# Attention with two kinds of heads, then a gated two-layer product: a new order for the first quarter, mask matmuls in row halves, and row loads put ahead of their transposes

## The chip, the core and the metric

The kernel runs on one core of a Trainium2 chip. TensorE (PE in the profile) multiplies, VectorE (DVE), ScalarE (ACT) and GpSimd (POOL) do the elementwise work, SyncE (SP) only issues transfers. Each engine takes its own instructions in the order in which the program wrote them and waits on semaphores for the others; a transfer is issued from the queue of one engine and lands later. The metric is the time of one execution in device microseconds (us); lower is better.

## The reference

For 4 batches, 8 heads, 768 positions and 64 values per head:

```
scores = (q @ k^T) / 8
mask   = causal                                  for the "retrieval" heads 0, 2, 6
       = causal and (key < 4 or distance < 64)   for the five "streaming" heads
a      = softmax(scores where mask, else -1e9)
x      = a @ v, heads side by side: [3072, 512]
h      = x @ w_in            # 512 -> 2048
out    = (h * sigmoid(beta * h)) @ w_out         # 2048 -> 512, [3072, 512] float32
```

## The kernel before

**Tiling.** The heads go in four pairs per batch, and the 768 query positions in two halves of 384 (3 tiles of 128). A *unit* is one pair of heads for one half of one batch; there are 32, and four units make a *chunk* (8 chunks, 384 rows of the output each). Of a pair, one head lies in partitions 0 to 63 and the other in 64 to 127, so that the scores of both come from two matmuls on 64 rows each that use the two halves of TensorE's rows side by side.

**Stages of a unit.** Its queries and keys are brought to the form [values, positions]. For the first 12 units this is done by a cast to bf16 (`cast`, words `ck`/`cq` in the table below), three transposes on TensorE (`transpose_qk`, `tk`/`tq`, L322) and a copy out of PSUM (`copy_qk`, `kk`/`kq`); later chunks are loaded already cast, row by row, from POOL's queue (`load_rows`, L282, into the tiles `s0` and `s1`), and transposed by transfers from SP's queue (`transposes_dma`, L294 for the keys, L297 for the queries). Streaming heads need a few key and value blocks with the sink positions in front (`KO`, `VO`; words `ko`, `vo`). Then `steps_QK` writes the scores to a two-bank PSUM tile `sp` (L451), ScalarE takes their exponentials into `es` (L460), and `steps_PV` multiplies by the values (L532; the extra 65th column gives the row sums). `normalize` divides, giving `x`, which is transposed into `xT`.

**Masks.** Units 0 to 7 have their masks added before the exponential: a matmul with the identity puts -1e9 where a key must not count (L422, words `ad`), and the scores are accumulated on it. Unit 5 is an exception: its words `ma` multiply `es` by a 0/1 mask on VectorE, as all units from 8 on do (L478 and following).

**The two layers.** `steps_G1` gives 128 groups of four 384-wide matmuls (L600), each followed by a tanh on ScalarE (L605) and a gate on VectorE (L608); `steps_G2` gives the output in steps of four 512-wide matmuls (L653). Groups 0 to 3 of chunk 0 read the first quarter of `w_in`, groups 4 to 7 the second. The quarters come by transfers from POOL's queue (L140, words `wi0` to `wi3`; `w_out` by `wo0` to `wo3`, L144).

**What sets the order.** All engines are scheduled by hand: instructions are issued as the program is written. `RAMP` is a list of words that writes out the work of units 0 to 7 and what goes between; `do(word)` turns each into instructions. `zz3` issues three 512-wide matmuls on zeros (`keep_busy`, L513) and `idle(9, ...)` nine more at the start (L167); they compute nothing. `lq1.0g` loads queries and keys of chunk 1, `lv` values, `mm`/`mA`/`mb` feed one step of the two layers, and a last letter v, a or g names the engine VectorE, ScalarE or GpSimd. `PLAN` has one row per unit from 8 on: V is a visit (scores and exponentials of two or three tiles), p a step of products with the values, a, A and b a step of the layers. `later(delay, fn)` puts smaller work (row loads, casts of values, masks) on a heap that `step` empties by a running estimate of TensorE's time.

## Time and profile before

| what | us |
|---|---|
| time, median of 3 runs (lowest, highest) | 228.91 (228.22, 229.04) |
| span of the profiled execution, first to last instruction | 227.0 |
| TensorE busy in it | 219.4 (97%) |
| ScalarE, VectorE, GpSimd busy | 154.0, 142.1, 87.3 |

The profiled execution's own time is not shown apart from its span; the median of the runs is 1.9 us longer than that span. In the profile's rows "busy" of TensorE counts a matmul from its start to the end of its result, so matmuls that follow each other overlap, and the distance from start to start is the better price of one. In rows of the timeline the first number is the start, the second the time covered, and a bracket tells how long the engine stood idle and what ended it.

### The profile page before, as it was taken

To read this page: it belongs to the slowest core of one execution; us is meant where nothing else is said; L and a number is where in the kernel's file an instruction comes from. 1 tells how busy PE (TensorE), PEld (TensorE's weight loads), DVE (VectorE), ACT (ScalarE), POOL (GpSimd) and SP (SyncE) were. 2 spreads that over 40 slices of the span, in tenths; PEclk is the share of its full clock that TensorE was granted. 3 is DMA by queue.
4 is the path that set the end of the run, shared out by engine and by line. 5 is a ranking of instruction groups with operands and counts; after the bars stand their busy time and mean duration, and the time that the engine had idled before them with its cause. 6 is when DMAs were issued, how large, how long until landed. Compare 5 with 4: busy or idle time off the path is not lost.

```text
span 227.0 us, 5019 instructions
## 1 busy us (share of the span) xinstructions
PE 219.4 (97%) x1898; PEld 126.4 (56%) x1917; DVE 142.1 (63%) x342; ACT 154.0 (68%) x254; POOL 87.3 (38%) x143
## 2 busy tenths in 40 slices
PE   7989999999999999999999999999999999999994
PEld 3555766654655665556654664556645655456553
DVE  4679888852684779357932699646963779028600
ACT  2698898946767897449933887569876878139621
POOL 5377952249163399143064049910670000000000
PEclk9999999999999999999999999999999999999999
DMA  6999999999999899989869779596963030111012
GB/s 204 262 301 239 225 197 198 195 220 171 149 216 178 161 153 144 141 175 133 103 131 162 126 151 140 92 133 103 216 64 107 24 81 0 49 46 46 0 49 92
DMA packets 95383, 31.66 MB, mean 139 GB/s; under 512 B 81776, under 2 KB 92416, under 8 KB 95360
## 3 DMA queue, kind: packets, MB, share of 16 engines
q1 hardware_dynamic: 58880, 22.82, 50.2%
q0 software_dynamic: 35904, 8.13, 41.9%
q10 hardware_dynamic: 576, 0.40, 0.6%
q8 instruction: 15, 0.25, 0.5%
q14 instruction: 8, 0.07, 0.1%
HBM read 27.27 MB, written 6.29 MB: 148 GB/s over the span
## 4 chain that ended last, share of the span: by engine, by line
PE 89%; DMA 4%; DVE 2%; SPq 2%; issue 1%; ACT 0%; ACTq 0%; DVEq 0%
PE mm L653 34%; PE mm L600 25%; PE sp L600 12%; PE sp L451 6%; PE po L532 6%; DMA s<-in_k_dram 3%; DMA s<-in_q_dram 2%; PE mm L638 2%; DVE es L478 1%; PE mm L322 1%; SPq L132 1%; PE mm L570 1%; PE mm L451 1%; SPq L119 1%; PE sp L422 1%
## 5 line engine op out<-in xcount | busy, mean ns | idle before, releaser
L653 PE MATMUL mm<-w_out_sb,gT 128*128 128x512 bf16 x349 | 84.1, 379 | 1.3 <-issue 0.5
L460 ACT ACTIVATE es<-sp 128x768 bf16<-128x768 f32 (+2 forms) x72 | 56.5, 837 | 19.6 <-PE sp L451 19.4
L600 PE MATMUL mm<-xT,w_in_sb 128*128 128x384 bf16 x348 | 64.6, 326 | 0.0
L600 PEld LDWEIGHTS <-w_in_sb 128*128 128x128 bf16 x512 | 47.8, 98 | 29.7 <-issue 0.2
L605 ACT ACTIVATE th<-mm,beta_h 128x384 f32<-128x384 f32 x87 | 49.8, 588 | 5.6 <-PE mm L600 0.9
L653 PEld LDWEIGHTS <-gT 128*128 128x128 bf16 x368 | 33.4, 98 | 36.0 <-issue 1.5
L608 DVE SCALAR_TENSOR_TENSOR gT<-th,mm 128x384 bf16<-128x384 f32 x87 | 46.8, 551 | 7.4 <-ACT th L605 3.8
L282 POOL DMA_DIRECT2D s<-in_q_dram x30 | 22.4, 761 | 27.2 <-DMA QTD<-s 21.7
L600 PE MATMUL sp<-xT,w_in_sb 128*128 128x384 bf16 x164 | 32.3, 326 | 0.0
L657 ACT ACTIVATE osb<-mm 128x512 f32<-128x512 f32 x23 | 13.8, 602 | 26.1 <-PE mm L653 25.8
L532 PEld LDWEIGHTS <-es 128*128 128x128 bf16 x472 | 23.3, 98 | 13.6 <-issue 1.5
L608 DVE SCALAR_TENSOR_TENSOR gT<-th,sp 128x384 bf16<-128x384 f32 x41 | 22.3, 552 | 5.6 <-ACT th L605 3.7
L532 PE MATMUL po<-VX,es 128*128 128x65 bf16 x360 | 24.9, 194 | 0.8 <-ACT VX L251 0.4
L605 ACT ACTIVATE th<-sp,beta_h 128x384 f32<-128x384 f32 x41 | 23.8, 586 | 2.3 <-PE sp L600 0.2
L282 POOL DMA_DIRECT2D s<-in_k_dram x30 | 22.4, 759 | 6.8 <-DMA w_out_sb<-in_moe_w_out_dram 5.2
L251 POOL CAST VX<-vs 128x512 bf16<-128x512 f32 x16 | 10.6, 662 | 34.6 <-DMA vs<-in_v_dram 31.8
L541 DVE RECIPROCAL rec<-po 128x6 f32<-128x6 f32 x28 | 5.4, 193 | 27.0 <-PE po L532 27.0
L478 DVE TENSOR_TENSOR es<-es,Mh 128x768 bf16<-128x768 bf16 (+1 forms) x26 | 17.4, 698 | 5.0 <-ACT es L460 4.4
L451 PE MATMUL sp<-QTD,KT 64*128 64x128 bf16 (+2 forms) x258 | 19.2, 240 | 0.6 <-ACT QTD L333 0.3
L545 DVE TENSOR_TENSOR x<-po,rec 128x384 bf16<-128x384 f32 x28 | 15.6, 557 | 1.0
L451 PEld LDWEIGHTS <-KT 64*128 64x128 bf16 x278 | 11.1, 94 | 5.8 <-issue 3.6
L259 POOL COPY VO<-VX 128x512 bf16<-128x512 bf16 x16 | 10.0, 649 | 7.3 <-DVE VX L251 7.3
(74 smaller groups left out, 157.2 us busy)
## 6 DMA issues: line engine op xcount, KB each, us to landing
vs<-in_v_dram SPq DMA_DIRECT2D x24, 256.0 KB, 5.5
out_dram<-osb SPq DMA_DIRECT2D x23, 256.0 KB, 2.8
w_in_sb<-in_moe_w_in_dram POOLq DMA_DIRECT2D x4, 512.0 KB, 9.7
w_out_sb<-in_moe_w_out_dram POOLq DMA_DIRECT2D x4, 512.0 KB, 16.5
s<-in_k_dram POOLq DMA_DIRECT2D x30, 64.0 KB, 4.8
s<-in_q_dram POOLq DMA_DIRECT2D x30, 64.0 KB, 5.1
s<-in_k_dram SPq DMA_DIRECT2D x4, 384.0 KB, 6.8
s<-in_q_dram SPq DMA_DIRECT2D x4, 384.0 KB, 8.6
```

Source lines behind the costliest of these rows:

```text
L251: copy(out=VX[b % 2][:, h2 * HT + t, :, 0:D], in_=staged["v", c][:, t])
L282: nc.gpsimd.dma_start(out=ROWS[c % 2, name][:, t, i * 4 * D:(i + 1) * 4 * D].rearrange("p (h d) -> p h d", d=D), in_=src[b, i:H:2, r:r + 1 ...
L451: nc.tensor.matmul(sps[i][r][:, x * 128:y * 128], key(a, lhs), s["QT"][half(a), qi * 128:(qi + y - x) * 128], start=first, stop=first or y ...
L460: nc.scalar.activation(out=views[i].rearrange("p r k j -> p r (k j)"), in_=banks[2][:, :, 0:n * 128], func=ACTF.Exp, scale=scale)
L478: nc.vector.tensor_mul(ev[:, :, 0:n], ev[:, :, 0:n], Mh[h2][:, None, m0:m0 + n].to_broadcast([128, 2, n, 128]))
L532: nc.tensor.matmul(po[:, qi, hh, :], e, val, start=(j == 0), stop=(j == len(lst) - 1))
L545: nc.vector.tensor_mul(xg[g][:, :, :, u % 2, :].rearrange("p a t d -> p t a d"), po[:, :, :, 0:D], rec.to_broadcast([128, HT, 2, D]))
L600: nc.tensor.matmul(hp[:, 0:HALF], w_in_sb[:, mo, fi * 128:(fi + 1) * 128], xT[c][:, mo, :], start=(mo == 0), stop=(mo == MO - 1))
L605: nc.scalar.activation(out=th, in_=hp[:, 0:HALF], func=ACTF.Tanh, scale=beta_h[:, fi:fi + 1])
L608: nc.vector.scalar_tensor_tensor(out=gTs[c][:, fi, :], in0=th, scalar=1.0, in1=hp[:, 0:HALF], op0=ALU.add, op1=ALU.mult)
L653: nc.tensor.matmul(op, gTs[c][:, fi, ns * 128:(ns + 1) * 128], w_out_sb[:, fi, :], start=(fi == 0), stop=(fi == FO - 1))
L657: nc.scalar.activation(out=osb, in_=op, func=ACTF.Copy, scale=0.5)
```

## The change

The first part of the program is written anew. The main points, with the names of the diff:

- Casts: the first units cast keys and queries in one instruction (`cast_both`, word `cb`), and all casts now run over heads outermost.
- Masks of units 0 to 7 (now unit 5 too): the -1e9 patterns are built on GpSimd in four kinds (`Nq`), folded into halves of 64 partitions (`Nt`, word `fo`), and added by matmuls of 64 columns (or two times 64) on 64 rows, alternating between the two row halves. The 0/1 masks that later units use are built later, on GpSimd (`late_masks`, word `mh`).
- Matmuls on zeros: five at the start (`zi5`) and 18 by `zz`, where there were nine and nine; the tile of zeros is smaller.
- `RAMP` and `PLAN` have their words in another order, and of the weights the third quarter of `w_in` goes ahead of, and the fourth behind, the first quarter of `w_out`.
- `transposes_dma` first issues all row loads of its chunk that are still on the heap. Before, four row loads of queries of chunk 6 and three of chunk 7 were still there when the transposes that read them were issued.
- `transpose_two` and `copy_two` are new, and no word of the table calls them.

```diff
+    def late_masks(part):
+        if part == 0:
+            nc.gpsimd.memset(Mh[0][:, 0:3], 1.0)
+            nc.gpsimd.memset(Mc, 1.0)
...
+    def folded(some, copy):
+        for r in range(2):
+            for h in range(2):
+                copy(out=Nt[64 * r:64 * r + 64, h, some], in_=Nq[64 * h:64 * h + 64, some])
...
-        copy(out=s["qkb"][:, "qk".index(name)], in_=staged[name, c, p // 2][:, p % 2:4:2].rearrange("p h t d -> p t h d"))
+        copy(out=s["qkb"][:, "kq".index(name)].rearrange("p t h d -> p h t d"), in_=staged[name, c, p // 2][:, p % 2:4:2])
...
+        for f in due_rows.pop(c, []):
+            f()
         for t in range(HT):
...
+    def cast_both(u, copy):
+        c, p = u // NPAIR, u % NPAIR
+        s = st_u.setdefault(u, {})
+        s["qkb"] = att.tile([128, 2, HT, 2, D], BF16, name="qkb", bufs=4)
+        copy(out=s["qkb"].rearrange("p i t h d -> p i h t d"), in_=both_of[c, p // 2][:, :, p % 2:4:2])
...
-                neg = Nc[:, 0:n * 128] if m is None else Ns[:, m * 128:(m + n) * 128]
-                nc.tensor.matmul(sps[i][r][:, 0:n * 128], ident, neg, start=True, stop=False)
+                kinds = [(0, 0, n)] if m is None else [((2, 3, 1, 3, 1)[m + x], x, 1) for x in range(n)]
+                todo.append([(r, h, *y) for y in kinds for h in range(2)])
                 covered[i, r] = n
+            opened_ = set()
+            while any(todo):
+                for some in todo:
+                    if some:
+                        r, h, kind, x, n = some.pop(0)
+                        rows_ = slice(64 * r, 64 * r + 64)
+                        nc.tensor.matmul(sps[i][r][:, x * 128:(x + n) * 128].rearrange("p (n j) -> p n j", n=n)[:, :, 64 * h:64 * h + 64], Nt[rows_, h, kind],
+                                         ident[rows_, None, 64 * r:64 * r + 64].to_broadcast([64, n, 64]), start=(r not in opened_), stop=False)
+                        opened_.add(r)
...
-        ck0g ne1 lv0.0 lv0.1 tk0 ck2a ne0 cq0v ck1a zz3 tq0 kq0a zz3 ad0.0 on0v lv0.2 kk0v cq1v tq1 qk0.0 tk2 ad0.1
+        zi5 cb0v cb1v zz1 zz2 zz3 fo0a lv0.0 ne0 tq0 fo1v tq1 tk0 zz1 lv0.1 zz2 lv0.2 kk0v tk1 zz1 ck3v lq1.0g zz2
+        be kq1a ad0.1 cb2v ad0.0 kq0a cq3a qk0.0 cv0.0v zz2 qk0.1 kk1a tq2 on0v kq2v cv0.1v zz2 ko1 tk2 cv0.2v vo0
...
-                later(1000 + 1500 * x, f)
+                due_rows.setdefault(c, []).append(later(1000 + 1500 * x, f))
```

Three places show how instructions moved; numbers behind a name tell buffers apart.

At the program's start VectorE before has these rows (`Mh`, `Ns`, `Mc` are masks, `qkb` the cast queries and keys, `s` the loaded ones):

```order
L150 MEMSET warm 1x1
L157 MEMSET zeros 128x256
L161 CAST idb<-idf 128x128
L177 MEMSET Mh_129 128x384
L193 TENSOR_SCALAR Ns<-Mh_129 128x256
L191 TENSOR_SCALAR Mc<-Nc 128x128
L193 TENSOR_SCALAR Ns<-Mh_129 128x384
L246 CAST qkb<-s_87 128x384
L228 MEMSET VX_145 128x48
L229 MEMSET VO_147 128x32
L330 COPY KT_149<-mm 128x384
```

And in the change:

```order
L149 MEMSET zeros 128x64
L155 MEMSET warm 1x1
L164 CAST idb<-idf 128x128
L328 CAST qkb<-s_89 128x2x2x3x64 x2
L212 COPY Nt<-Nq 64x384 x4
L377 COPY KT_126<-mm 128x384
L264 CAST qkb<-s_94 128x2x3x64
L742 TENSOR_SCALAR beta_h<-mm 128x16
```

The first masks left VectorE, the first two casts take four tiles each, and four copies that fold masks stand between them and the first copy of transposed keys.

GpSimd, around the transfers of the second quarter of `w_in`, before (the casts are those of chunk 1's last unit):

```order
L228 MEMSET VX_146 128x48
L229 MEMSET VO_148 128x32
L246 CAST qkb<-s_244 128x384
L312 COPY KO_156<-KT_150 128x128
L312 COPY KO_157<-KT_150 128x128
L140 DMA w_in_sb<-in_moe_w_in_dram 128x4x512 x3
L251 CAST VX_146<-vs 128x8x64
```

And in the change:

```order
L328 CAST qkb<-s_273 128x2x2x3x64
L173 AFFINE_SELECT Mh_111<-Mh_111 128x2x128
L173 AFFINE_SELECT Mh_111<-Mh_111 128x128
L187 MEMSET Mh_111 4x256
L359 COPY KO_133<-KT_127 128x128
L359 COPY KO_134<-KT_127 128x128
L173 AFFINE_SELECT Mh_111<-Mh_111 128x2x128
L173 AFFINE_SELECT Mc<-Mc 128x128
L253 COPY Mh_111<-Mh_111 128x256
L141 DMA w_in_sb<-in_moe_w_in_dram 128x4x512 x2
L269 CAST VX_123<-vs 128x8x64
L145 DMA w_out_sb<-in_moe_w_out_dram 128x4x512
```

The building of the 0/1 masks moved into this stretch, ahead of the second and third quarters of `w_in`, and the first of `w_out` took the fourth quarter's place.

SP, the transposes of chunk 6 before, with the semaphores that each row waits for (DMASW are those of POOL's row loads):

```order
L294 DMA_TRANSPOSE KT_149<-s_665 128x4x128 [waits DMAHW0_49,DMASW7_49,DMASW1_49]
L297 DMA_TRANSPOSE QTD_144<-s_643 128x4x128 [waits DMASW3_49,DMAHW1_49,DMASW2_49,PE_49]
L297 DMA_TRANSPOSE QTD_144<-s_643 128x4x128 [waits DMAHW2_49,PE_49]
L297 DMA_TRANSPOSE QTD_144<-s_643 128x4x128 [waits DMAHW3_49,PE_49]
L132 DMA vs<-in_v_dram 128x8x64 [waits DMAHW4_49]
```

And in the change:

```order
L316 DMA_TRANSPOSE KT_126<-s_624 128x4x128 [waits DMAHW2_49,DMASW1_49,DMASW0_49]
L319 DMA_TRANSPOSE QTD_121<-s_779 128x4x128 [waits DMASW3_49,DMAHW3_49,DMASW2_49,PE_49]
L319 DMA_TRANSPOSE QTD_121<-s_779 128x4x128 [waits DMASW5_49,DMAHW4_49,DMASW4_49,PE_49]
L319 DMA_TRANSPOSE QTD_121<-s_779 128x4x128 [waits DMASW7_49,DMAHW5_49,DMASW6_49,PE_49]
L133 DMA vs<-in_v_dram 128x8x64 [waits DMAHW6_49]
```

All three transposes of queries now wait for row loads, where two did not.

More of the change, by code (lines that the diff above doesn't have):

```diff
@@ L145, in load_w_out @@
         w_done.add(i)
+    zeros = consts.tile([128, 128], BF16, name="zeros")
+    nc.vector.memset(zeros, 0.0)
+    still = zeros[:, None, :].to_broadcast([128, 4, 128])
     load_qk(0, 0, 2)
@@ L166, in idle @@
             nothing = pool.tile([128, 512], F32, name=name)
-            nc.tensor.matmul(nothing, zeros[:, 0:128], zeros, start=True, stop=True)
-    idle(9, ps_m, "mm")
+            nc.tensor.matmul(nothing.rearrange("p (n j) -> p n j", n=4), zeros, still, start=True, stop=True)
     def select(buf, cm, step_, base, n):
@@ L448, in rows @@
                 seq = runs[0] + runs[1]
+            ends = {r: (r, x, y) for r, x, y, e in seq}
             for r, x, y, (a, lhs, qi, val, diag, m) in seq:
-                first = x >= covered.get((i, r), 0)
+                whole = (i, r) not in covered
                 nc.tensor.matmul(sps[i][r][:, x * 128:y * 128], key(a, lhs), s["QT"][half(a), qi * 128:(qi + y - x) * 128],
-                                 start=first, stop=first or y == covered[i, r])
+                                 start=whole, stop=whole or (r, x, y) == ends[r])
         def soft(i):
@@ L512, in keep_busy @@
         for i in range(n):
-            nc.tensor.matmul(sums_bank(0), zeros[:, 0:128], zeros, start=True, stop=True)
+            nc.tensor.matmul(sums_bank(0).rearrange("p (n j) -> p n j", n=4), zeros, still, start=True, stop=True)
     def steps_PV(u):
@@ L755, in do @@
         elif what == "ml":
-            late[n].pop(0)()
+            late[n].pop(0)(copies[eng or "v"])
         elif what == "tt":
             run(steps_T(n))
+        elif what == "zi":
+            idle(n, ps_m, "mm")
         elif what == "zz":
@@ L797 @@
+        mm ro3 mm mm ro3 mA mA mb mb tt8 mb mb mb
     """
```

156 lines of the change are left out of this document (94 added, 62 removed).

## The prediction

> **What bounds the kernel now.** I read the chain of waits first, then busy time by stretches.
>
> ```profile
> PE 89%; DMA 4%; DVE 2%; SPq 2%; issue 1%; ACT 0%; ACTq 0%; DVEq 0%
> ```
>
> ```profile
> 0.00:5.00 5.00, 3.71 (x10) 1.32 (x11) 1.86 (x8) 1.49 (x2) 3.25 (x15) 1.00 0.62 184
> 5.00:10.00 5.00, 4.66 (x47) 2.89 (x45) 3.30 (x10) 3.23 (x6) 0.86 (x3) 1.00 1.23 274
> 10.00:15.00 5.00, 4.43 (x64) 2.49 (x63) 3.45 (x8) 3.69 (x7) 4.19 (x11) 1.00 1.12 308
> 15.00:22.00 7.00, 6.61 (x99) 4.07 (x98) 6.42 (x16) 5.99 (x11) 4.78 (x11) 1.00 1.24 245
> 22.00:27.50 5.50, 5.50 (x81) 3.94 (x78) 4.75 (x12) 4.83 (x8) 5.44 (x11) 1.00 1.19 229
> 27.50:46.00 18.50, 18.50 (x121) 11.25 (x119) 15.73 (x30) 16.71 (x29) 6.52 (x10) 1.00 1.22 197
> 145.00:223.70 78.70, 78.17 (x640) 45.40 (x646) 42.95 (x102) 49.24 (x81) 11.46 (x15) 1.00 0.45 78
> ```
>
> Behind each stretch stand its length and then the busy time of TensorE, of its weight loads, of VectorE, ScalarE and GpSimd, the granted clock, the share of the DMA engines and GB/s. TensorE carries 89% of the chain. From 22 us on it is full; what waits is the ramp ahead of that, and there the DMA engines are full as well (shares over 1). A changed order can therefore gain in two ways only: the dense part begins earlier, or it holds less. Two starts mark how far the ramp has come, the first group of the first layer and the fifth, the first that reads the second quarter of `w_in`. The rows of TensorE:
>
> ```profile
> 1.29 3.83 PE L167 MATMUL mm<-zeros 128*128 128x512 bf16 x9 [1.29 <-DVE zeros L157]
> 4.96 0.33 PE L322 MATMUL mm<-idb,qkb 128*128 128x128 bf16 x3
> 7.40 0.34 PE L451 MATMUL sp<-QTD,KT 64*128 64x128 bf16 x4 [0.34 <-ACT QTD L333]
> 22.00 1.80 PE L600 MATMUL mm<-xT,w_in_sb 128*128 128x384 bf16 x10
> 27.50 1.46 PE L600 MATMUL sp<-xT,w_in_sb 128*128 128x384 bf16 x8
> 142.12 0.24 PE L532 MATMUL po<-VX,es 128*128 128x65 bf16 x2 [0.36 <-DVE es L478]
> ```
>
> First scores come at 7.40, the first group at 22.00, the fifth at 27.50. Behind that I use one wait, 0.36 at 142.12 for a masked exponential.
>
> **The ramp.** The second quarter of `w_in` is issued on GpSimd's queue; these are its rows there, and behind them the time to landing of the first and the second quarter:
>
> ```profile
> 11.55 0.87 POOL L140 DMA_DIRECT2D w_in_sb<-in_moe_w_in_dram  x1
> 16.66 0.51 POOL L246 CAST qkb<-s 128x384 bf16<-128x384 f32 x1 [0.30 <-DMA s<-in_q_dram]
> 19.89 2.23 POOL L140 DMA_DIRECT2D w_in_sb<-in_moe_w_in_dram  x3
> ```
>
> ```profile
> w_in_sb<-in_moe_w_in_dram POOLq DMA_DIRECT2D x1, 512.0 KB, 9.3
> ```
>
> ```profile
> w_in_sb<-in_moe_w_in_dram POOLq DMA_DIRECT2D x1, 512.0 KB, 7.0
> ```
>
> The first lands at 11.55 + 9.3 = 20.9, the second at 19.89 + 7.0 = 26.9, 0.6 before the fifth group: the weights come just in time today, so a faster ramp meets them. In the change GpSimd has other work ahead of that issue. Prices by form:
>
> ```profile
> L171 POOL TENSOR_SCALAR_AFFINE_SELECT Mh<-Mh 128x256 bf16<-128x256 bf16 x2 | 0.8, 408 | 0.8 <-DVE Mh L177 0.7
> L180 POOL MEMSET Mh<- 4x256 bf16 x1 | 0.3, 302 | 0.1
> L171 POOL TENSOR_SCALAR_AFFINE_SELECT Mh<-Mh 128x128 bf16<-128x128 bf16 x1 | 0.3, 295 | 0.0
> L312 POOL COPY KO<-KT 128x128 bf16<-128x128 bf16 x6 | 1.7, 299 | 1.8 <-ACT KT L330 1.5 <-DVE KT L330 0.3
> ```
>
> The load that GpSimd waits for at 16.66 is the same, and I let it land at the same time, since it stands behind as many loads in SP's queue and the DMA engines are full there. Then one cast of two tiles (two single ones are 2 x 0.51; joined, an estimate of 0.85), selects 0.41 + 0.30, memset 0.30, two copies of keys 0.60, selects 0.41 + 0.30, a copy of 256 columns 0.30 to 0.40: 3.5 in all. The issue comes at 16.66 + 3.5 = 20.2, 0.3 later than before, and with the same 7.0 it lands at 27.2. The ends for 7.0: 9.3 of the first quarter above, and below it 3.4, the distance at which queued transfers of this size follow each other further down.
>
> ScalarE paces the rest. Its rows ahead of and behind the first group:
>
> ```profile
> 19.25 2.01 ACT L460 ACTIVATE es<-sp 128x768 bf16<-128x768 f32 x3
> 21.12 0.83 ACT L579 COPY xT<-mm 128x768 bf16<-128x768 bf16 x1
> 21.80 1.57 ACT L460 ACTIVATE es<-sp 128x768 bf16<-128x768 f32 x2
> 23.19 1.23 ACT L605 ACTIVATE th<-mm,beta_h 128x384 f32<-128x384 f32 x2
> ```
>
> From start to start three exponentials take 1.87 and the copy 0.68. In the change the load that lands at 16.4 is cast (0.5) and its transposes copied (0.5), so ScalarE comes at 17.4 to a copy of `xT` (0.7), three exponentials (1.9) and a shorter one (at most 0.6): 20.6. With masks and scores (0.4) the first group starts near 21.0, a us sooner than before. From there TensorE had 5.5 of dense work to the fifth group; four products and some mask columns fewer make an estimated 4.9 to 5.5 of it, so TensorE is there at 25.9 to 26.5. The weights are not: the fifth group starts at about 27.25. **-0.25.**
>
> Fillers, first scores and casts lie ahead of this and I cost them at nothing. Nine fillers at the start become five and end about 1.7 earlier (3.67 from 1.29 to 4.96, over nine, is 0.41 each); 18 later ones cost TensorE 18 x 0.21, where nine did. The first scores come later: both first casts (VectorE) take four tiles, behind them stand folds, and I place the first scores at about 8.5 against 7.40. The cover is the load at 16.4, since all chains meet again there; were it gone, the 1.1 would count. For the casts:
>
> ```profile
> L246 DVE CAST qkb<-s x9: 529/543/554, 4.9 to 58.7; 128x384 bf16<-128x384 f32 x9
> L251 DVE CAST VX<-vs x7: 415/422/653, 21.2 to 67.3; 128x512 bf16<-128x512 f32 x7
> ```
>
> A cast of 512 columns that writes its values in the order of heads takes 422 ns, one of 384 whose tiles are outermost 543. Heads outermost should bring the latter to about 330 (by columns from the first), and two tiles to 0.6; the other end is 2 x 0.54 = 1.1 for the first two, 1.0 together on VectorE, which delays first scores to 9.5 and still leaves them inside the cover. The Trainium skill, "VectorE: DVE Perf Modes", section "What auto-detection actually checks", says that a mode of double speed needs an outermost size even or equal on both sides. By that the old casts, three tiles outermost, miss it and the new ones, two heads, take it: about 0.6 instead of 1.1, with the same sum.
>
> **Masks.** The rows of a full mask pair, of scores on row halves, and of matmuls with new weights each:
>
> ```profile
> 17.43 0.34 PE L451 MATMUL sp<-QTD,KT 64*128 64x128 bf16 x6
> 17.70 0.30 PE L532 MATMUL mm<-VX,es 128*128 128x65 bf16 x4
> 17.83 0.33 PE L322 MATMUL mm<-idb,qkb 128*128 128x128 bf16 x3
> 23.70 0.48 PE L422 MATMUL sp<-Ns,idb 128*128 128x384 bf16 x2
> 24.02 0.28 PE L532 MATMUL po<-VX,es 128*128 128x65 bf16 x4
> ```
>
> Two full masks take 0.32 to the next start, 0.16 for 384 columns; 28 of them, 7,424 columns, cost 3.1 in all. The change has 124 half ones, 62 pairs, nearly all of 64 columns. Three pairs of 128 columns took 0.27, so 0.09 a pair; half by columns is 0.045, and 62 of those 2.8. That is my value, the nearest row. Below, 62 x 0.03 = 1.9, if a pair costs what one of the four products at 17.70 costs (0.13 for four). Above, 124 x 0.057 = 7.1, if halves don't overlap and each costs what one of the three at 17.83 does (0.17 for three). So masks gain 0.3, or 1.2, or lose 4.0, all ahead of the fifth group, where TensorE has 0.7 to 1.3 to spare: 0.
>
> The Trainium skill, "TensorE: Matmul & The Clock Gate", section "LDWEIGHTS (loading the stationary operand)", gives a load of weights by its columns alone, 128 / 1.2 = 107 ns, whatever the rows. By it the 124 loads would take 13.3 us in a row. The row at 17.70, four new weights in 0.13, contradicts it as a price on the path.
>
> **Behind the ramp.** Four products come after the fifth group instead of before it: 4 x 0.03 = **+0.1**. Unit 5's masking leaves VectorE (two multiplies that were off the path). The slots of `PLAN` stand in another order with the same words per unit; of the wait of 0.36 I take half, **-0.2**, with 0 and the whole as ends. The fourth quarter of `w_in` now takes the place of the first of `w_out`. Rows of GpSimd, which waits in turn for each landing:
>
> ```profile
> 34.37 0.75 POOL L282 DMA_DIRECT2D s<-in_k_dram  x1 [1.55 <-DMA w_in_sb<-in_moe_w_in_dram]
> 37.76 0.74 POOL L282 DMA_DIRECT2D s<-in_k_dram  x1 [2.64 <-DMA w_out_sb<-in_moe_w_out_dram]
> 41.09 0.74 POOL L282 DMA_DIRECT2D s<-in_k_dram  x1 [2.59 <-DMA w_out_sb<-in_moe_w_out_dram]
> ```
>
> The weights land 3.4 apart; the fourth place came shortly before 37.76, with 0.3 added at 37.8 or so. Its first reader, 16 groups of four matmuls (4 x 0.16) and a few products behind the fifth group, is due at about 38. So 0, with 0.5 as the dear end.
>
> The row loads put ahead of the transposes of chunks 6 and 7 delay those transposes and what stands behind them on SP:
>
> ```profile
> 128.54 3.81 SPq L297 DMA_TRANSPOSE QTD<-s  x3
> 132.84 1.48 POOL L282 DMA_DIRECT2D s<-in_q_dram  x2 [10.97 <-DMA QTD<-s]
> 140.18 0.61 PE L451 MATMUL sp<-QTD,KT 64*128 64x384 bf16 x8
> ```
>
> GpSimd stood 10.97 waiting for those transposes before it could load late rows; now it issues them first, at 0.75 each, four and three of them, 3.0 at most. Their issue ends at 132.35, and the visit that reads the result starts at 140.18, so some 3 us of delay are hidden, and so are a load of values and a store behind them. Cover gone, it would be 3.0. I cost it 0.
>
> **Sum.** -0.25 + 0.1 - 0.2 = -0.35 on the profiled span of 227.0, so 226.65; with the 1.9 by which the median of the runs stands above that span, 228.5.
>
> **Rivals.**
> Faster: the weights come early and TensorE's own work decides. Issue at 20.2 and 5.7 instead of 7.0 suffice. For it: 3.4 from transfer to transfer shows what the queue can do; against it, DMA shares of 1.2 throughout and 9.3 for the first. The fifth group would start at 25.95: -1.55 + 0.1 - 0.2 = -1.65, time 227.2.
>
> Slower: the half masks don't overlap, so TensorE becomes the bound. At 7.1 its work ahead of the fifth group grows by 4.0, and it comes there at 25.9 + 4.0 = 29.9, +2.4, time 231.2. It decides from 1.3 of extra work on, 0.07 a pair. For it: weights of 128 columns are loaded for a matmul of only 64, and the pair's loads may wait for each other. Against: 0.09 for a pair with twice the columns.
>
> The slots: visits need a free score tile, so an exponential of 0.8 must have ended. With fewer products between two visits TensorE waits for ScalarE; two or three such waits make 2.0, time 230.5. For it: every row of the table has its words in another order; against: ScalarE is busy 49.2 of 78.7 in the last stretch.
>
> That the row loads do nothing for the time is part of the forecast, since their wait is off TensorE's path.
>
> **Chances.** The forecast has 0.56 (its own range 227.8 to 229.5: the weights half a us earlier or later, the dear end of the fourth quarter), the faster rival 0.18, half masks 0.13, slots 0.13. Half a per cent, 1.14 us, is about what a measurement can tell from no change: below 227.8 lie the faster rival and 0.02 of the forecast, 0.20; within, 0.54 and a tenth of the slots, 0.55; above, the rest, 0.25. The range reaches from 227.0, under the faster rival, to 230.7, over the slots; half masks at the full price (0.13) lie outside.
>
> **What would show it.** Right: the fifth group starts near 27.2, just behind the landing of its weights, with TensorE idle some 1 us ahead of it; mask pairs under 0.07 from start to start; the two joined casts at about 0.6; GpSimd without the wait of 10.97. Wrong: TensorE dense up to the fifth group (then masks or scores bound it), a fifth group before 26.5, or waits of TensorE on score tiles behind 46 us.

## The result and the profile after

| | before | changed |
|---|---|---|
| time, median (lowest, highest), 7 runs each | 228.83 (228.22, 229.04) | 232.06 (229.81, 236.05) |
| ratio of the two, 95% interval | | 1.0109 (1.0079 to 1.0138) |
| span of the profiled execution | 227.0 | 234.3 |

The change made the kernel slower, by 1.1% in the ratio and by 1.4% in the medians, and it made its time uncertain: its first seven runs lay within 0.8 us of each other before, and within 6.2 us after (over all experiments, some hundred runs, the kernel before reached from 228.0 to 231.2). Every ratio here leaves out runs of a kernel that lie over 1.5% above its fastest, so 236.05 counts in the median and not in the ratio. The trace that follows is that of this longest run; a second trace, of a run of 232.61, comes with the experiments.

What TensorE waited for in the changed kernel (in all, times, longest):

```profile
PE sp L658 <- DMA w_in_sb<-in_moe_w_in_dram: 4.3, 1, 4.3
PE mm L170 <- DVE warm L155: 1.1, 1, 1.1
PE mm L711 <- issue: 0.5, 3, 0.2
PE mm L369 <- ACT KT L377: 0.5, 1, 0.5
PE mm L369 <- DVE qkb L328: 0.5, 1, 0.5
```

And its chain of waits by engine:

```profile
PE 84%; DMA 11%; ACT 1%; issue 1%; POOL 1%; SPq 0%; DVE 0%; ACTq 0%
```

DMA has 11% of the chain, where it had 4%. The rows of TensorE at the first, the fifth and the ninth group of the first layer:

```profile
22.21 1.82 PE L658 MATMUL mm<-xT,w_in_sb 128*128 128x384 bf16 x10
...
31.81 1.46 PE L658 MATMUL sp<-xT,w_in_sb 128*128 128x384 bf16 x4 [4.29 <-DMA w_in_sb<-in_moe_w_in_dram]
...
37.71 1.46 PE L658 MATMUL mm<-xT,w_in_sb 128*128 128x384 bf16 x8
```

And the ninth group before:

```profile
30.44 0.81 PE L600 MATMUL mm<-xT,w_in_sb 128*128 128x384 bf16 x4
```

The first group is 0.21 later than before, the fifth 4.31, the ninth 7.27. Stretches of the same trace (length, busy time of TensorE, weight loads, VectorE, ScalarE, GpSimd, granted clock, share of the DMA engines, GB/s):

```profile
22.00:27.50 5.50, 5.50 (x98) 3.86 (x91) 5.22 (x16) 4.96 (x9) 5.44 (x10) 1.00 1.13 221
27.50:30.80 3.30, 0.02 (x1) 0.00 (x0) 0.69 (x2) 0.85 (x2) 1.91 (x3) 1.00 1.17 208
30.80:31.80 1.00, 0.00 (x0) 0.00 (x0) 0.00 (x0) 0.00 (x0) 0.00 (x0) 0.51 1.20 190
31.80:37.60 5.80, 5.79 (x26) 3.27 (x27) 2.64 (x6) 1.74 (x3) 1.94 (x3) 0.50 1.22 196
37.60:46.00 8.40, 8.40 (x54) 4.99 (x52) 6.58 (x13) 7.27 (x13) 2.16 (x3) 1.00 1.22 196
```

So the loss has two parts. TensorE stood 4.3 us for the second quarter of `w_in`; and 3.3 us into that wait the granted clock went to 0.50 and stayed there for 5.8 us behind its end, which cost another 2.9 (5.8 us of work at half the clock). From the ninth group on the two traces run in step: the last matmul comes 6.83 later, so the rest of the kernel gained 0.44.

The issue of the quarter on GpSimd's queue, and its way to landing:

```profile
17.40 0.82 POOL L328 CAST qkb<-s 128x768 bf16<-128x768 f32 x1 [0.81 <-PE po L590]
18.18 0.65 POOL L173 TENSOR_SCALAR_AFFINE_SELECT Mh<-Mh 128x256 bf16<-128x256 bf16 x2
18.89 0.30 POOL L187 MEMSET Mh<- 4x256 bf16 x1
19.28 0.53 POOL L359 COPY KO<-KT 128x128 bf16<-128x128 bf16 x2
19.76 0.41 POOL L173 TENSOR_SCALAR_AFFINE_SELECT Mh<-Mh 128x256 bf16<-128x256 bf16 x1
...
20.71 1.50 POOL L141 DMA_DIRECT2D w_in_sb<-in_moe_w_in_dram  x2
```

```profile
w_in_sb<-in_moe_w_in_dram POOLq DMA_DIRECT2D x1, 512.0 KB, 11.1
```

Issued 0.8 later than before, it took 11.1 us instead of 7.0. The trace says where they went: the semaphore of such a transfer counts up 16 times, as often as the core has DMA engines, and the reader starts just behind the last count (at 31.81 for 31.76). I call each count the landing of a *share*. Times of the fifteenth and the last share, from the semaphore's events, for the second load of chunk 1's queries (the load that the prediction let the ramp meet again at) and for this quarter:

```
                                     queries        second quarter of w_in
                                     15th   last    issue  15th   last
before                               16.28  16.54   19.89  26.71  26.94
changed                              16.60  17.28   20.71  27.66  31.76
changed, second trace                16.32  17.40   20.82  28.34  29.49
before, weights 1.0 later            16.68  16.70   20.87  26.89  27.83
changed, old slots                   16.15  17.55   20.99  28.17  30.13
same, full masks                     16.11  16.19   20.06  27.74  27.88
changed, old slots, masks behind     16.25  17.79   20.28  27.31  27.42
none of the three                    16.05  16.10   18.99  26.65  27.49
same, fourth quarter ahead           16.23  16.55   19.29  26.01  26.25
same, half masks                     17.02  17.40   19.88  26.44  28.67
```

The fifteenth share came 0.95 later than before, the last 4.8. One share that lags is not new with the change. Three experiments below alter the kernel before elsewhere (its row loads, its slots, its fourth quarter) and leave this issue at 19.56 to 19.97; in their traces the quarter took 7.5, 7.9 and 8.0 us, its last share 1.3 to 1.5 behind the fifteenth, and landed at 27.47 to 27.69, just as the fifth group was due. The 7.0 of the first trace was a good landing.

### The profile page after: what moved, and what is told of

The parts are those of the page before. It is cut to its first block, busy times and chain, and to the rows that moved or that the text cites. A ratio compares the mean times of both kernels' runs of the same rounds, so it can differ in the third digit from the quotient of the medians.

```text
span 234.3 us, 5230 instructions
## 1 busy us (share of the span) xinstructions
PE 222.6 (95%) x1999; PEld 127.8 (55%) x2018; DVE 142.5 (61%) x344; ACT 155.7 (66%) x258; POOL 86.8 (37%) x140
## 4 chain that ended last, share of the span: by engine, by line
PE 84%; DMA 11%; ACT 1%; issue 1%; POOL 1%; SPq 0%; DVE 0%; ACTq 0%
PE mm L711 34%; PE mm L658 23%; PE sp L658 12%; DMA s<-in_q_dram 6%; PE po L590 6%; PE sp L509 6%; DMA w_in_sb<-in_moe_w_in_dram 5%; PE mm L696 2%; PE mm L509 1%; PE mm L369 1%; PE mm L628 1%; ACT qkb L264 0%; POOL KO L359 0%; ACT KT L377 0%; SPq L120 0%
## 5 line engine op out<-in xcount | busy, mean ns | idle before, releaser
L711 PE MATMUL mm<-w_out_sb,gT 128*128 128x512 bf16 x349 | 85.0, 379 | 1.3 <-issue 0.5
L658 PEld LDWEIGHTS <-w_in_sb 128*128 128x128 bf16 x512 | 48.7, 99 | 35.6 <-DMA w_in_sb<-in_moe_w_in_dram 4.5
L518 ACT ACTIVATE es<-sp 128x768 bf16<-128x768 f32 (+2 forms) x72 | 56.4, 836 | 15.7 <-PE sp L509 15.5
L658 PE MATMUL mm<-xT,w_in_sb 128*128 128x384 bf16 x344 | 65.5, 328 | 0.0
L711 PEld LDWEIGHTS <-gT 128*128 128x128 bf16 x368 | 32.8, 98 | 33.6 <-issue 1.1
L658 PE MATMUL sp<-xT,w_in_sb 128*128 128x384 bf16 x168 | 35.5, 340 | 4.3 <-DMA w_in_sb<-in_moe_w_in_dram 4.3
L663 ACT ACTIVATE th<-sp,beta_h 128x384 f32<-128x384 f32 x42 | 24.4, 585 | 9.9 <-PE sp L658 6.8
L269 POOL CAST VX<-vs 128x512 bf16<-128x512 f32 x13 | 8.5, 653 | 50.3 <-DMA vs<-in_v_dram 42.7
L666 DVE SCALAR_TENSOR_TENSOR gT<-th,sp 128x384 bf16<-128x384 f32 x42 | 23.1, 553 | 5.5 <-ACT th L663 3.0
L536 DVE TENSOR_TENSOR es<-es,Mh 128x768 bf16<-128x768 bf16 (+1 forms) x24 | 13.5, 589 | 6.9 <-ACT es L518 6.2
L277 POOL COPY VO<-VX 128x512 bf16<-128x512 bf16 x16 | 10.9, 701 | 11.1 <-DVE VX L269 11.1
```

The costliest lines, as they stand in the source:

```text
L277: copy(out=vo[:, i - 1, :, 0:D], in_=vx[:, i, :, 0:D])
L518: nc.scalar.activation(out=views[i].rearrange("p r k j -> p r (k j)"), in_=banks[2][:, :, 0:n * 128], func=ACTF.Exp, scale=scale)
L536: eng.tensor_mul(ev[:, :, 0:n], ev[:, :, 0:n], Mh[h2][:, None, m0:m0 + n].to_broadcast([128, 2, n, 128]))
L658: nc.tensor.matmul(hp[:, 0:HALF], w_in_sb[:, mo, fi * 128:(fi + 1) * 128], xT[c][:, mo, :], start=(mo == 0), stop=(mo == MO - 1))
L663: nc.scalar.activation(out=th, in_=hp[:, 0:HALF], func=ACTF.Tanh, scale=beta_h[:, fi:fi + 1])
L666: nc.vector.scalar_tensor_tensor(out=gTs[c][:, fi, :], in0=th, scalar=1.0, in1=hp[:, 0:HALF], op0=ALU.add, op1=ALU.mult)
```

## Experiments

All times are medians (lowest to highest) against the kernel before on the same chip, whose medians lay between 228.59 and 228.83; the interval is that of the ratio. The theory: **the lead of the weights over the fifth group is what the change took away**. Rivals: the half masks (through their number of instructions), and the slots or row loads.

**The weights far ahead.**

```diff
- lv2.2 cb7g no2 ...  mh2 mlg wi1 ex4.0 wi2
+ lv2.2 wi1 wi2 cb7g no2 ...  mh2 mlg ex4.0
```

> The changed kernel with the transfers of the second and third quarter of w_in issued ahead of the joined cast of unit 7 and the late masks on GpSimd, some 3 us earlier; all else stays. Theory (the fifth group waits for the weights, and what the change did was to take away 0.8 us of their lead): the quarter lands before 26.5, TensorE does not wait for it, the clock stays at 1.00, the runs agree within 0.5%, and the time is 227 to 228, under both kernels. Rival one (more instructions to load, by the half masks, hold back one DMA engine): that engine's share is late all the same, less than before but by 1 to 3 us past 27.5, the runs spread by over 1%, time 229 to 231. Rival two (the order of the slots or the row loads cost): 231 to 233 as the changed kernel.

236.38 (235.75 to 237.59), 1.0330 (1.0296 to 1.0364). The expectation fell. The quarter landed at 24.80, and TensorE waited all the same, for values:

```profile
29.05 0.44 PE L590 MATMUL po<-VX,es 128*128 128x65 bf16 x5 [3.82 <-DVE VX L269]
```

The DMA engines are full here (a share of 1.24 from 16.4 to 25 us), and 1 MB moved ahead by 4.3 us took their time from what stood there: the third load of chunk 1's values landed at 28.54, where it had landed at 23.63 in the changed kernel. The lead has a window, not a direction. The clock was lost as well: it fell to 0.50 at 28.16, 2.9 us after TensorE's last work, and stayed there for 6.8 us, so some of the 236.38 is clock and not wait.

**Full masks.** Units 0 to 7 get one matmul on 128 rows for each kind and tile.

```diff
-  matmul(sp[..., 64 * h:64 * h + 64], Nt[rows_, h, kind], ident[rows_, ...])   # r, h in turn
+  matmul(sp[...], Nq[:, kind], ident)
```

> The changed kernel with the masks of units 0 to 7 as full matmuls on 128 rows, one for two half ones or more, so that TensorE has some 100 matmuls and weight loads fewer to fetch; the order of words and the issue of the weights stay. Theory (the lead of the weights): still slow and still spread, 229 to 233, the fifth group 0.3 to 4 us after 27.5 behind the landing of w_in. Rival one (instruction fetches of the half masks): the last of the 16 shares lands with the others, the fifth group starts by 28.0, the runs agree within 0.5%, time 228.3 to 229.2.

230.60 (229.04 to 232.17), 1.0073 (1.0045 to 1.0100). Time and spread are those of the theory; the landing is that of the rival: in its trace, of its fastest run, the fifteenth and the last share land together, at 27.54 and 27.57, and the fifth group starts at 27.85 without a wait. These full masks are not those of the kernel before. They are 62 matmuls, where the kernel before has 28 wider ones and the change 124. From the start of each to the next start (or to its own end, where TensorE then stood idle) they take 5.24 us in all, the 28 take 4.25 and the 124 take 2.14. So wherever full masks stand in for half ones below, TensorE has 1.0 us more of masks than the kernel before.

**The same lateness without the change.**

```diff
-  ... tq6 wi1 qk5.0 ...
+  ... tq6 du wi1 qk5.0 ...      # du: two memsets of 384 columns on GpSimd
```

> The kernel before with two memsets of 384 columns (0.42 us each by the profile of the changed kernel) on GpSimd ahead of the issue of the second to fourth quarter of w_in, which so comes at about 20.7 instead of 19.9, as in the changed kernel; nothing else differs. Theory: the fifth group starts at the landing, 27.7 or later, 0.3 to 4 us behind before; runs spread by over 1%; time 229.2 to 233. Rival one (instruction fetches of the half masks): the landing moves by just the 0.8, TensorE waits 0.3, no spread, 228.9 to 229.4. Rival two (slots or row loads): as before, 228.9.

229.78 (228.66 to 233.40), 1.0033 (1.0009 to 1.0056). Nothing but the issue was moved, 0.98 later, and the median rose by 1.0. One of the twelve runs reached 233.40; the 29 of the kernel before beside them end at 230.26. TensorE in its trace, of a run of 228.80, one of its fastest:

```profile
27.31 0.50 PE L572 MATMUL mm<-idb,x 128*128 128x128 bf16 x6
27.87 0.83 PE L602 MATMUL sp<-xT,w_in_sb 128*128 128x384 bf16 x4
```

The fifth group starts 0.04 behind the last share (27.83). Taking away lead alone makes the kernel before slower, by 0.3%; what its longest run waited for no trace shows.

**Twice that lateness** (four memsets, issue at 21.85):

> The kernel before with four memsets (1.7 us) ahead of the issue of the quarters of w_in instead of the two of the run before (median 229.78, 228.66 to 233.4). Theory (what counts is the lead): the fifth group 1.0 us later again, median 230.5 to 231.5, and more runs in which the wait passes 3.7 us and the clock drops, the highest 233 to 237. Rival (the spread belongs to the runs of that batch, not to the lead): median 229.8 to 230.2, no wider.

230.62 (230.33 to 231.69), 1.0094 (1.0059 to 1.0128). The dose holds: 1.0 for 0.98, and 2.0 for 1.96. The long runs that were expected did not come: no clock under 1.00 among its six.

```profile
29.76 1.48 PE L602 MATMUL sp<-xT,w_in_sb 128*128 128x384 bf16 x8 [1.07 <-DMA w_in_sb<-in_moe_w_in_dram]
```

**The row loads alone**, in the kernel before:

```diff
-                later(1000 + 1500 * x, f)
+                due_rows.setdefault(c, []).append(later(1000 + 1500 * x, f))   # issued first by transposes_dma
```

> The kernel before with one part of the change alone: row loads of a chunk that are still on the heap are issued ahead of its transposes. Theory: the 10.97 us wait of GpSimd goes, the transposes of chunks 6 and 7 end up to 3 us later, and no instruction of TensorE starts later: 228.9, within 0.3%. Rival two (the row loads cost): the visits of chunks 6 and 7 wait for the transposed queries, up to 3 us each, 230 to 233.

228.76 (228.57 to 229.77), 0.9999 (0.9981 to 1.0016). They cost nothing.

**The late masks behind the weights**, in the changed kernel:

```diff
-  tq6 mh1 kk5v kk6a cx0a ko5 ko6 pv3 ex4.1 mh2 mlg wi1 ex4.0 wi2
+  tq6 kk5v kk6a cx0a ko5 ko6 pv3 ex4.1 wi1 ex4.0 wi2 mh1 mh2 mlg
```

> The changed kernel with the selects and the copy of the late 0/1 masks (2.0 us of GpSimd) behind the issue of the second and third quarter of w_in instead of ahead of it; the weights then go out at about 19.2, between the 20.7 of the changed kernel and the 16.4 that made TensorE wait 3.8 us for values. Theory (the lead of the weights over the fifth group): landing at 26 to 27, TensorE there at 27.4 and without a wait, clock 1.00, spread under 0.7%, 228.0 to 228.8. Rival (the DMA engines are full, and any place takes as much from the values or the weights): a wait of TensorE for values or keys of 1 us or more appears ahead of the fifth group, 229.5 to 233.

230.21 (229.27 to 232.00), 1.0077 (1.0046 to 1.0108). The expectation of 228.0 to 228.8 fell. In its trace, of its fastest run, the wait for weights went (landing at 26.21, fifth group at 28.0), but another stands ahead of the first group, for keys whose load has a late share (17.46):

```profile
18.48 0.33 PE L369 MATMUL mm<-idb,qkb 128*128 128x128 bf16 x3 [0.93 <-ACT KT L377]
```

**The slots alone**, in the kernel before (PLAN and row loads of the changed one):

> The kernel before with the slots of the changed kernel (PLAN) and its row loads ahead of the transposes; the first part (RAMP, masks, casts) stays as before. Theory (the slots gain what the changed kernel's trace gains behind 32 us, 7.27 less 6.83, and cost nothing): 228.3 to 228.6, the wait of 0.36 behind the masked exponentials at 142 gone. Rival (slots bring TensorE to wait for exponentials): 229.5 to 231.

229.75 (228.48 to 231.00), 1.0045 (1.0017 to 1.0072): the time is the rival's, the wait is another one, for transposed queries. TensorE, and GpSimd ahead of it:

```profile
94.83 0.51 PE L455 MATMUL sp<-QTD,KT 64*128 64x384 bf16 x8 [1.00 <-DMA QTD<-s]
```

```profile
75.86 1.49 POOL L282 DMA_DIRECT2D s<-in_q_dram  x2
82.48 0.69 POOL L251 CAST VX<-vs 128x512 bf16<-128x512 f32 x1 [5.13 <-DMA vs<-in_v_dram]
83.11 2.98 POOL L282 DMA_DIRECT2D s<-in_q_dram  x4
```

And the same visit before:

```profile
95.48 0.50 PE L451 MATMUL sp<-QTD,KT 64*128 64x384 bf16 x8
```

Before, this visit started 5.0 after the queries had landed (90.47). The new slots ask for it at 93.8; four loads of query rows stand on GpSimd's queue behind a cast that waits 5.1 us for values; the queries land at 94.69.

**Matmuls on zeros ahead of the fifth group**, in the changed kernel:

```diff
-  xx2 cx2a mA no6
+  xx2 cx2a zf12 mA no6      # zf12: 12 matmuls on zeros into one tile
```

> The changed kernel with 12 matmuls on zeros (2.6 us) right ahead of its fifth group, so that TensorE is not idle for as long while it waits for the weights. Theory (a long wait costs twice, since the granted clock drops to 0.50 some 3.7 us after TensorE's last work and for 5.8 us behind its return): the clock stays at 1.00 in all runs; the fifth group starts at 30.1, or at the landing where that is later; time 230.8 to 232.5, and no run over 233. Rival (the clock drops for another reason, load or heat): runs with a clock under 1.00 stay, and single ones reach 236 to 238.

234.28 (233.07 to 236.97), 1.0227 (1.0189 to 1.0265). Worse than no fill, and not clean. (The expectation's 3.7 is 3.3 in the changed kernel's trace, from 27.52 to 30.82.) In this trace the fillers first wait 0.73 for their tile, which a gate on VectorE still reads, and they hold TensorE until 32.41, beyond the landing at 30.07.

```profile
29.82 2.75 PE L835 MATMUL mm<-zeros 128*128 128x512 bf16 x12 [0.73 <-DVE gT L666]
32.41 0.81 PE L658 MATMUL sp<-xT,w_in_sb 128*128 128x384 bf16 x4
```

And the clock was lost elsewhere. The queries' last share came at 17.73, TensorE was busy for 64% of 16 to 20 us with no wait over 1.4, and then had 0.50 for 3.4 us, from 20.72 on, with TensorE busy all the while:

```profile
16.00:18.00 2.00, 1.39 (x32) 1.14 (x30) 1.36 (x4) 0.71 (x3) 0.32 (x3) 1.00 1.14 180
18.00:20.00 2.00, 1.18 (x22) 0.93 (x22) 0.60 (x2) 2.00 (x5) 1.84 (x6) 1.00 1.25 256
20.00:22.00 2.00, 1.85 (x36) 1.26 (x36) 1.64 (x4) 1.52 (x4) 2.00 (x7) 0.68 1.09 183
22.00:24.00 2.00, 2.00 (x31) 1.50 (x30) 1.30 (x6) 1.71 (x3) 1.94 (x3) 0.50 0.84 212
```

So one long wait is not the only way to lose it, and filling one wait does not keep it.

**Taking the three apart.** The changed kernel with the old slots; then with full masks; with the late masks behind the weights; with both.

> The changed kernel with the slots (PLAN) of the kernel before. By now three causes stand: the slots, which let a visit near 94 us wait for queries that are loaded behind a cast on GpSimd (1.1 in the kernel before with the new slots); the masks built ahead of the weights on GpSimd; and half masks, whose instructions are more, so that a 16 KB fetch of instructions on one DMA engine comes 1 to 2 us earlier, at 14.8 to 15.5, while that engine still has a share of the load that the whole ramp waits for. If all three count, this run loses the slots' 1.1 and keeps the rest: 230.2 to 231.3, spread over 1%, no wait of TensorE for transposed queries. If the slots did not count in the changed kernel: 231.5 to 232.5.

> The same with full masks instead of half ones: of the three causes only the late masks ahead of the weights on GpSimd are left. If the half masks' fetches count: the last share of the load of chunk 1's second queries lands within 0.3 of the other fifteen, and the time is 0.8 to 1.5 under the run with half masks and the old slots, 229.0 to 229.8. If they do not: within 0.4 of that run.

> The changed kernel with the old slots and with the late masks behind the weights on GpSimd: of the three causes only the half masks are left. If they count: the last share of that load still lands 0.7 or more behind the others in the profile, TensorE waits for keys ahead of the first group, and the time is 228.9 to 229.6. If they do not: 228.2 to 228.7.

> All three taken out: the changed kernel with the old slots, full masks, and the late masks behind the weights; what is left of the change is the new order of words, the casts with heads outermost, the fillers and the row loads. If the three causes are all: no wait of TensorE for weights or queries, spread under 0.6%, 228.0 to 228.8, level with the kernel before or a little under it. If another part costs (the casts, the order of the first words): 229.3 or more.

| old slots, and | time | ratio (interval) |
|---|---|---|
| half masks, late masks ahead | 232.05 (230.73 to 233.74) | 1.0156 (1.0124 to 1.0189) |
| full masks, late masks ahead | 230.24 (229.09 to 231.04) | 1.0065 (1.0041 to 1.0089) |
| half masks, late masks behind | 230.15 (229.68 to 231.09) | 1.0066 (1.0045 to 1.0086) |
| full masks, late masks behind | 229.69 (228.78 to 230.86) | 1.0030 (1.0007 to 1.0054) |

The old slots brought the changed kernel nothing, against the first expectation; in neither of the changed kernel's own two traces did the visit near 94 us wait. The next two came 0.4 and 0.5 above what was expected if half masks count, and the last took its other branch, 229.3 or more: another part costs too. Taking out either the half masks or the late masks ahead of the weights brings 0.9%; taking out the second as well brings only 0.35% more, with intervals that overlap. That fits two causes that eat the same lead, but the runs don't separate them further. TensorE with half masks, in the first and the third:

```profile
18.57 0.33 PE L369 MATMUL mm<-idb,qkb 128*128 128x128 bf16 x3 [1.22 <-ACT KT L377]
...
30.17 0.82 PE L658 MATMUL sp<-xT,w_in_sb 128*128 128x384 bf16 x4 [2.57 <-DMA w_in_sb<-in_moe_w_in_dram]
```

```profile
18.81 0.33 PE L369 MATMUL mm<-idb,qkb 128*128 128x128 bf16 x3 [1.38 <-ACT KT L377]
```

With neither, the fifth group is on time (27.54) and the fourth quarter is not; it lands 14.0 us after its issue at 25.50:

```profile
39.50 0.82 PE L653 MATMUL mm<-xT,w_in_sb 128*128 128x384 bf16 x4 [0.93 <-DMA w_in_sb<-in_moe_w_in_dram]
```

**The fourth quarter, and each cause alone.** The kernel with none of the three, and:

```diff
-  wi1 ex4.0 wi2 mh1 mh2 mlg ...  hf wi3 wo1
+  wi1 ex4.0 wi2 wi3 mh1 mh2 mlg ...  hf wo1
```

> The kernel without the three causes, and with the fourth quarter of w_in issued ahead of the first of w_out again, as in the kernel before. Theory (a fourth cause: in the trace without the three the fifth group was on time and TensorE waited 0.93 at 39.50 for the fourth quarter): no wait for weights, the 21st group within 0.3 of the kernel before, 228.1 to 228.8, spread under 0.6%. Rival (casts, fillers or the order of the first words cost what is left): 229.3 to 230, as without this edit.

> The same as the run with the fourth quarter ahead, but with half masks. Theory: their more numerous instructions bring the fetches of 16 KB to 14.8 to 15.5 and 20.2, the last share of chunk 1's second queries lands 0.7 to 1.7 behind the rest, TensorE waits about 1 us for keys ahead of the first group: 0.8 to 1.5 above the run with full masks. Rival (half masks are free, what they cost was the late quarters): within 0.4 of it.

> The same as the run with the fourth quarter ahead, full masks kept, but with the new slots. Theory from the kernel before with the new slots: 0.6 to 1.4 above the run with the old slots, with a wait of TensorE for transposed queries near 94 us. Rival (slots and the first part were made for each other, the wait comes of the mix): level or 0.3 to 0.5 under it.

| fourth quarter ahead, and | time | ratio (interval) |
|---|---|---|
| full masks, old slots | 229.94 (229.28 to 230.80) | 1.0041 (1.0018 to 1.0064) |
| half masks, old slots | 230.66 (229.37 to 232.08) | 1.0085 (1.0055 to 1.0115) |
| full masks, new slots | 230.39 (229.63 to 230.81) | 1.0063 (1.0040 to 1.0086) |

The fourth quarter's wait went and the time did not: the expectation of 228.1 to 228.8 fell, and some 0.4% stays that none of the named causes explains. Its trace, of a run at the median, shows where most of it lies: its span is 1.0 longer than before, the fifth group starts 0.63 later and the last matmul 0.62 later, so TensorE loses its 0.6 ahead of the fifth group. There it is nearly full from the first group to the fifth, 5.8 us against 5.5 before, and starts that stretch 0.28 later:

```profile
22.30:28.10 5.80, 5.59 (x81) 3.92 (x80) 4.94 (x13) 4.38 (x8) 4.72 (x10) 1.00 1.18 213
```

So with these full masks the new order leaves TensorE no shorter way to the fifth group. The masks themselves are a rival for what stays, since they take 1.0 more than those before; no run tests it with the masks of before. Half masks add 0.7 and new slots 0.45 in the medians, both a little less than the theory had (0.8 and 0.6 at least), and the intervals overlap; for the slots the trace shows the mechanism again (1.1 for transposed queries).

**The fourth quarter late, alone**, in the kernel before:

```diff
-  kk7v wi2 kq7v wi3 cx1a ...  mm wo0 pv4
+  kk7v wi2 kq7v cx1a ...  mm wo0 wi3 pv4
```

> The kernel before with the fourth quarter of w_in issued behind the first of w_out, alone. Theory: it lands at 37.5 or later, 15 of its shares and then the last one, against a need at about 38.3; the median rises by 0.1 to 0.6, and runs with a late share reach 230 to 231. Rival (0.3 or more of slack always hides it): within 0.1% of before.

228.40 (228.19 to 228.84), 0.9988 (0.9974 to 1.0001). No cost there, as the rival had it: the quarter lands at 38.01, in time.

**A version to beat both:** the last one, and the second quarter ahead of two copies of keys.

```diff
-  kk5a ko5 ko6 ad5.1 tq6 wi1 qk5.0
+  kk5a wi1 ko5 ko6 ad5.1 tq6 qk5.0
```

> A try for something better than both: the kernel before with the fourth quarter of w_in behind the first of w_out (228.40 by itself) and the second quarter issued ahead of the copies of keys for which GpSimd waits 1.5 us, so some 1.5 us earlier. Theory (lead of the weights): TensorE does not wait for weights even where the last share is 1 us late, 228.0 to 228.4, no run above 229. Rival (the values of chunk 1 come later by the bytes that go ahead of them, as where the weights went out 4 us earlier): a wait for values ahead of the first groups, 229 to 232.

228.84 (228.22 to 231.64), 1.0001 (0.9959 to 1.0042). It beats nothing: in its trace the quarter goes out 2.0 earlier than before and lands at 26.27, but two of its twelve runs are over 231, and one of the kernel before beside them is 231.2. So the weights' issue is not the only thing that makes a run long.

**The changed kernel again.**

> The changed kernel once more, for a second trace and more runs beside the kernel before. Theory: median 230.5 to 232.5, spread 229.5 to 236; in the trace chunk 1's second queries land 0.5 or more behind fifteen of their shares, the fifth group starts at the landing of w_in between 28 and 32, and the visit near 94 us waits if the fifth group started by about 28.5.

233.18 (230.03 to 233.94), 1.0110 (1.0040 to 1.0181). The shares and the fifth group are as expected, the median is 0.7 above. In its trace, of a run of 232.61, the fifth group waits 1.35 and starts at 29.54, at the landing (29.49). A wait of another kind costs as much, later on:

```profile
155.22 0.48 PE L658 MATMUL mm<-xT,w_in_sb 128*128 128x384 bf16 x2 [1.57 <-DMA xT<-x]
```

The transposed `x` landed at 155.17 here; before, it landed at 152.93 for a group at 153.29. The visit near 94 us did not wait in this trace.

## Why the prediction was wrong

**The step that failed** is in the ramp: "with the same 7.0 it lands at 27.2". The issue was half a us off, 20.71 for 20.2, and TensorE came to the fifth group at 27.5 rather than at 25.9 to 26.5; with the 7.0 this would have been a wait of 0.2. But the transfer took 11.1 and 8.7 us in the two traces, and 7.5 to 8.0 in three more of the kernel before, so 7.0 was the low end of what it takes even there. The prediction had seen that the weights come "just in time today" and named 9.3 as the upper end of the term; then it did not carry that end into its range or into a rival, although 9.3 alone gives a landing at 29.5 and a time near 230.8. That the lead was the term is shown by moving the issue alone: 0.98 later cost 1.0, 1.96 later cost 2.0.

**A second step** failed with it: the load of chunk 1's queries "is the same, and I let it land at the same time". It landed at 17.28 and 17.40 instead of 16.54, since one share of 16 was late, and with it ScalarE's copy of `xT` started at 18.14 where 17.4 stood. That is 0.7 of the 1.2 by which the first group was late, 22.21 for 21.0. The other half a us is in the chain behind the copy: 4.07 from there to the first group, where the sum had 3.6. With full masks and the load on time the copy did start at 17.3 to 17.5, and the first group still came at 22.0 to 22.2, with more masks on TensorE.

**A cost that stood nowhere**: the clock. In the longest run a wait of 4.3 us was worth 7.2, because the clock was halved for 5.8 us behind it. The first rows of the prediction showed clocks of 1.00 throughout, and no term asked what a long wait would do to it. Of the first seven runs the three longest have a mean clock under 1 (0.985 to 0.993); the median one, 232.06, has 1.00, so this cost is not what moved the median.

**The rivals.** Slower by half masks that do not overlap: wrong as a mechanism. Twelve of them take 0.18:

```profile
12.03 0.35 PE L478 MATMUL sp<-idb,Nt 64*128 64x64 bf16 x12
12.21 0.33 PE L509 MATMUL sp<-QTD,KT 64*128 64x256 bf16 x4
```

That is 0.03 a pair, the cheap end of the term (0.045 was taken). On TensorE all 124 take 2.14 where the 28 took 4.25, a gain of 2.1; the sum had 3.1 and 2.8. They cost by late transfers, not on TensorE: taking them out, with all else kept, put the load's shares together and brought 0.9% (with the old slots). The slots: the waits that were named, for score tiles, did not come behind 46 us; slots do cost, 1.1 in the kernel before, by asking earlier for queries that come by transfers. One trace with the new slots also waits 1.57 for transposed `x`; no run shows that the slots did this. The faster rival needed the weights in 5.7 us and got 11.1.

**What held.** The joined casts take 0.56 and the single ones mostly 0.36, where 0.6 and 0.33 stood:

```profile
L328 DVE CAST qkb<-s x3: 548/559/559, 3.9 to 9.1; 128x768 bf16<-128x768 f32 x3
L264 DVE CAST qkb<-s x6: 350/362/545, 8.2 to 66.0; 128x384 bf16<-128x384 f32 x6
```

The first scores came at 9.04 (8.5 stood), the row loads cost nothing, the wait of 10.97 on GpSimd is gone, and behind the ninth group the trace gains 0.44 where 0.2 stood. The fourth quarter's dear end, 0.5, is real once the ramp is early: 0.93 in one trace.

**What stays open.** Why one share in 16 of that load is late with half masks: in all eight traces with them the queries' last share lands 0.4 to 1.5 behind the fifteenth, in the five of the new ramp with full masks 0.05 to 0.32. Their instructions are more, and packets of 16 KB on the instruction queue come early, at 14.2 to 15.5, each 1.1 to 1.2 us long; but with full masks they came at 15.2 to 15.7, which overlaps, so the time of that packet alone does not tell the two apart. Why the last share of the quarter itself came 4.1 late in one run, 1.2 in another and 0.2 to 1.5 in the kernel before is open too. The 0.4% that stays without all named causes was not taken apart, nor what the clock costs without the wait.

## What to carry to other kernels

Where a transfer lands 0.6 us ahead of its reader and the DMA engines are full, count every step that delays its issue as on the path, however idle the issuing engine looks; and moving it ahead can take the time from another transfer (4.3 us here cost the values 4.9), so look for the window rather than for "earlier". Price a transfer by the spread of its landings in the trace (the last of its 16 shares), not by the one landing seen, and carry both ends into the range. Ask of a long wait of TensorE what it does to the clock: here the clock fell to half in waits of 4.29 and 3.82 us and stayed there for 5.8 and 5.9 us behind their end, which for the first cost 2.9 more; in one of 2.57 us it did not fall.

## What was not expected of the hardware

One share of 16 can run late by the same amount in transfer after transfer: the one that was 4.1 behind the fifteenth at 31.76 was followed by ones 3.6 behind at 34.92, 38.33 and 41.64, the next transfers of GpSimd's queue to land. It did not catch up in those 10 us, with the DMA engines full. This looks like one engine that lags behind the other fifteen, but the trace does not name the engine of a share.

The clock fell 3.3 us after TensorE's last work (27.5 to 30.8) and came back 6.8 later, 5.8 us into full work. With the weights far ahead it fell 2.9 after the last work, again for 6.8. With the matmuls on zeros it fell with TensorE 64% busy (54% in the last 3.4 us) and came back after 3.4. The Trainium skill, "TensorE: Matmul & The Clock Gate", section "Part 1: The HAM clock gate (the "warmup" mystery)", tells of a free-running window of about 3.4 us, and of one idle window for the way down. The trace agrees with the length, 3.4 and twice that; but the case with the matmuls on zeros had no idle window. How empty a stretch must be stays open: in the changed kernel with the old slots one of 3.4 us with TensorE 25% busy, around its wait of 2.57, left the clock at 1.00.

The Trainium skill, "Runtime: NRT & Kernel Launch", section "Instruction fetch mechanics", says that instructions come in blocks of 16 KB and that the cost of crossing a block is mostly hidden. The traces agree with the size; whether such a packet, on DMA engines that are full, delays the share behind it is what stays open above.
